# Seven block products for eight in the second down projection of a two-layer gated network (fp32, one NeuronCore)

## The chip, the cores and the metric

The kernel runs on one NeuronCore of a Trainium2 chip. The metric is the device time of one execution in microseconds; the time before is the median of three runs. The profile is one further execution, taken by the hardware profiler. Engines are named as in the profile: PE is TensorE, PEld its weight loads, DVE VectorE, ACT ScalarE, POOL GpSimd, SP the engine whose queue issues every DMA of this kernel.

## What is computed

An attention over 32 memory slots feeds a three-way maximum layer ("moe") and then a gated layer ("moe2"). The change lies in the gated layer alone, 4608 tokens, d_model 512, d_ff 1536:

```python
def _moe_ref(x, w1, w2, w3, w_out) -> np.ndarray:
    h = np.maximum(np.maximum(x @ w1, x @ w2), x @ w3)
    return (h @ w_out).astype(np.float32)
...
def _moe2_ref(x, w_gate, w_val, w_out) -> np.ndarray:
    gate = 1.0 / (1.0 + np.exp(-(x @ w_gate)))
    val = x @ w_val
    return (gate * val @ w_out).astype(np.float32)
```

All data are fp32.

## The kernel before

**Numbers.** Each fp32 operand of a large product is held as two fp32r tiles, a rounded part and what is left of it (`w_split`, L133: a ScalarE copy, then a subtraction on GpSimd or VectorE), and a product is three matmuls (`PASSES`, L333: low x high, high x low, high x high).

**First part (to about 568 us).** Attention, then the maximum layer, in four passes over pairs of batches. Its result x2 goes to DRAM (`x2_step`, L388). During the passes the weights of the gated layer are unpacked and kept in DRAM (`wbf`). In the last pass the first chunk's x and the first weights of the gated layer are prepared (L593 to L605).

**Second part: the gated layer.** Tokens go in five chunks (`SUPER`, L421), each of two halves of 512 tokens, in the last two chunks 384. For each chunk a loop over j (L776) takes the twelve column blocks of 128 of d_ff in six pairs, j and j + 6. The product of x (two halves of tokens, two halves of d_model) with the gate and value weights of such a pair is made in seven block products instead of eight (Strassen, in the form of Winograd): `x_sums` and `x_split` (L505, L515) make the seven left sides once per chunk, `t_make` (L460) makes the seven right sides from the weights in the first chunk and stores them in DRAM (`tbs`), `t_load` (L480) reads them in the later chunks. `up` (L724) makes one of the seven products for the gate (v = 0) or the value (v = 1) in PSUM, in the order 1, 6, 2, 7, 5, 4, 3, and the sums that belong to it. Each of the four blocks (c: half of the tokens, h: half of the pair) ends in `block_done` (L702): the sigmoid on ScalarE for the gate, gate x value on VectorE into `gf`, then a copy on ScalarE and a subtraction on GpSimd into the split tile `gg` (L720 to L722).

**The down projection.** `down` (L749) multiplies gg with w_out for 128 tokens at a time: two h, three passes, six matmuls with 128x128 weights (gg) and 512 columns (w_out) into one PSUM tile `po`. In the first j a ScalarE copy takes it to `acc`, in later j VectorE adds it to `acc`, and in the last j each 128x512 tile goes to `out`. So the sums over f are kept per 128 tokens, 8 or 6 tiles. w_out is split once per j in the first chunk (`wo_make`, L476), stored in `wos`, and loaded again later (`wo_load`, L484); it shares a ring of 11 buffers (`q4`, L419) with the seven right sides.

**Order.** The products of one j are run one j later, in between: after the third of the fourteen `up` calls each is followed by one `down` (L779 to L785). The preparation of the next weights stands behind each `up` pair, that of the next chunk's x in the last j of a chunk (L790 to L794). From this program order the framework's planner builds the order on each engine ahead of the run, by due times that it works out itself; it moves instructions past others where tiles and buffers allow. On the chip each engine then takes its own list in order, and SP its DMAs.

## Time and profile before

| | |
|---|---|
| median of 3 runs | 1390.36 us (1390.21 to 1392.23) |
| the profiled execution, as timed | 1393.86 us |
| its span, first to last instruction | 1392.1 us |
| mean granted TensorE clock | 0.984 |
| second part: first matmul to the end | 568.8 to 1392.1 us |
| gg @ w_out: matmuls, busy time of TensorE | 1296, 327.8 us |
| GpSimd on gg (120 operations) | 143.8 us |
| VectorE on acc (180 operations) | 124.3 us |

How to read the lines: a group is "line engine op, out<-in, shapes xcount | busy us, mean ns of one | idle time before them and what ended it". A line of the timeline begins with the start and the duration in us. A line of the waits has the total time, the number of waits and the longest. A line of the windows has, for each engine in the order PE, PEld, DVE, ACT, POOL, the busy time and the number of instructions in the window, then the granted clock, the share of the DMA engines and GB/s. Many operations are recorded at a helper's line: L73 is `sub`, L134 the copy in `w_split`; there the tiles tell what it is.

### The profile page before, as it was taken

Reading aid. Unit: us, or ns where it says so; the run is one execution under the profiler, and the core shown is the slowest. Engines: PE = TensorE matmul, PEld = TensorE weight load, DVE = VectorE, ACT = ScalarE, POOL = GpSimd, SP = SyncE. Lnnn points to the kernel's source line nnn. Section 1 sums busy time; section 2 is a strip of 40 time slices with the busy share of each in tenths; the row PEclk is TensorE's granted clock in tenths of the full one; section 3 lists DMA queues with packets and bytes.
Section 4 is the critical chain, followed back from the end, with each engine's and each line's share of the span. In section 5 each row is a group of like instructions: output and inputs, shape, how many; then the busy total and the mean of one; then the engine's idle time right before and its main releaser. Section 6 shows DMA issues by size and latency. Waiting matters only on the chain.

```text
span 1392.1 us, 22135 instructions
## 1 busy us (share of the span) xinstructions
PE 1338.2 (96%) x7864; PEld 1185.0 (85%) x7864; DVE 873.1 (63%) x1549; ACT 570.8 (41%) x1204; POOL 517.4 (37%) x454
## 2 busy tenths in 40 slices
PE   6588999999999999899999999999999999999998
PEld 3487899999999989688888888888888899999997
DVE  5999748976985897567765344454444544554454
ACT  5687546645654663353343321332222322133221
POOL 2776512331341228454486111371112711161111
PEclk8799999999999999999999999999999999999999
DMA  9588658767757745865556554465455666566661
GB/s 309 190 281 301 204 176 269 250 215 248 235 164 254 232 154 172 301 242 212 204 186 229 177 176 158 156 205 193 158 178 166 218 224 218 194 229 235 216 212 61
DMA packets 112271, 292.44 MB, mean 210 GB/s; under 512 B 12577, under 2 KB 28961, under 8 KB 112161
## 3 DMA queue, kind: packets, MB, share of 16 engines
q1 hardware_dynamic: 112160, 291.03, 62.1%
q8 instruction: 62, 1.02, 0.3%
q14 instruction: 49, 0.39, 0.1%
HBM read 224.92 MB, written 66.06 MB: 209 GB/s over the span
## 4 chain that ended last, share of the span: by engine, by line
PE 79%; DVE 10%; DMA 5%; issue 2%; ACT 2%; POOL 1%; SPq 0%; DVEq 0%; ACTq 0%; POOLq 0%
PE po L755 21%; PE px L688 16%; PE pz L688 11%; PE pv L688 10%; PE ps L393 8%; PE ps L370 8%; DVE g L73 2%; PE ps L343 2%; DVE ca L129 1%; DVE ca L128 1%; PE ps L209 1%; DVE hm L381 1%; DVE hm L382 1%; PE ps L246 1%; DVE ca L127 1%
## 5 line engine op out<-in xcount | busy, mean ns | idle before, releaser
L755 PE MATMUL po<-wo,gg 128*128 128x512 f32 x1296 | 327.8, 392 | 1.3 <-POOL gg L73 1.3
L73 POOL TENSOR_TENSOR gg<-gf,gg 128x512 fp32r<-128x512 f32 (+1 forms) x120 | 143.8, 1199 | 471.4 <-ACT gg L721 430.6
L755 PEld LDWEIGHTS po<-wo,gg 128*128 128x128 f32 x1296 | 242.4, 188 | 49.8 <-POOL gg L73 1.7
L370 PE MATMUL ps<-attn,g 128*128 128x288 f32 x1728 | 255.0, 301 | 19.4 <-DVE g L73 12.4
L370 PEld LDWEIGHTS ps<-attn,g 128*128 128x128 f32 x1728 | 243.3, 192 | 28.4 <-issue 11.4
L688 PE MATMUL px<-xa,tb 128*128 128x512 f32 (+1 forms) x1080 | 246.3, 370 | 6.2 <-DVE x L70 6.2
L767 DVE TENSOR_TENSOR acc<-po,acc 128x512 f32<-128x512 f32 x180 | 124.3, 690 | 176.5 <-PE po L755 176.3
L688 PEld LDWEIGHTS px<-xa,tb 128*128 128x128 f32 x1080 | 199.8, 189 | 34.9 <-issue 6.4
L688 PE MATMUL pv<-xa,tb 128*128 128x512 f32 (+1 forms) x720 | 169.2, 367 | 0.0
L688 PE MATMUL pz<-xa,tb 128*128 128x512 f32 (+1 forms) x720 | 169.2, 367 | 0.0
L73 POOL TENSOR_TENSOR h<-hm,h 128x288 fp32r<-128x288 f32 x96 | 83.6, 876 | 207.6 <-DVE h L70 105.6
L393 PE MATMUL ps<-h,wo 128*128 128x288 f32 x1152 | 159.1, 297 | 0.6 <-DVE hm L382 0.6
L393 PEld LDWEIGHTS ps<-h,wo 128*128 128x128 f32 x1152 | 155.3, 190 | 2.7 <-issue 1.9
L688 PEld LDWEIGHTS pz<-xa,tb 128*128 128x128 f32 x720 | 132.4, 188 | 18.8
L688 PEld LDWEIGHTS pv<-xa,tb 128*128 128x128 f32 x720 | 131.8, 188 | 17.7
L721 ACT CAST gg<-gf 128x512 fp32r<-128x512 f32 (+1 forms) x120 | 69.4, 578 | 177.8 <-DVE gf L717 132.4
L739 DVE TENSOR_TENSOR u<-pz,p 128x512 f32<-128x512 f32 (+1 forms) x120 | 76.3, 636 | 101.9 <-PE pz L688 97.8
L73 DVE TENSOR_TENSOR g<-ps,g 64x384 fp32r<-64x384 f32 x180 | 99.2, 552 | 33.2 <-ACT g L357 30.2
L711 ACT ACTIVATE sg<-sg 128x512 f32<-128x512 f32 (+1 forms) x90 | 53.1, 590 | 143.4 <-DVE sg L709 143.1
L357 ACT CAST g<-ps 64x384 fp32r<-64x384 f32 x192 | 90.6, 474 | 37.3 <-DVE g L73 22.9
L73 POOL TENSOR_TENSOR xa<-xf,xa 128x512 fp32r<-128x512 f32 (+1 forms) x64 | 79.3, 1261 | 21.4 <-ACT xa L134 18.7
L717 DVE TENSOR_TENSOR gf<-gf,sg 128x512 f32<-128x512 f32 (+1 forms) x90 | 72.3, 803 | 10.6 <-DVE gf L716 1.4
(92 smaller groups left out, 1402.4 us busy)
## 6 DMA issues: line engine op xcount, KB each, us to landing
tb<-tbs SPq DMA_DIRECT2D x168, 512.0 KB, 3.8
wx<-wxs SPq DMA_DIRECT2D x72, 384.0 KB, 4.0
wo<-wos SPq DMA_DIRECT2D x48, 512.0 KB, 5.0
tbs<-tb SPq DMA_DIRECT2D x42, 512.0 KB, 2.8
raw<-wb_dram SPq DMA_DIRECT2D x48, 384.0 KB, 3.6
kv<-kvm_dram SPq DMA_DIRECT2D x48, 256.0 KB, 4.8
raw<-wx_dram SPq DMA_DIRECT2D x24, 384.0 KB, 3.9
wxs<-wx SPq DMA_DIRECT2D x24, 384.0 KB, 4.3
```

The lines of the kernel that those rows point to most:

```text
L73: eng.tensor_tensor(out=o, in0=a, in1=b, op=ALU.subtract)
L343: pe.matmul(ps[:, :384], lhsT=vt[:, x, 2 * e:2 * e + 2].rearrange("p a m -> p (a m)"), rhs=w[:, y], start=(n == 0), stop=(n == 2),)
L357: act.copy(t[r, 0], ps[r, :384])
L370: pe.matmul(ps[w][:, :U], lhsT=G[b, j, g][:, x, 128 * w:128 * w + 128], rhs=at[:, y, hf * U:hf * U + U], start=(n == 0), stop=(n == 5),)
L393: pe.matmul(ps[:, :U], lhsT=wo1_t[:, x, (d * J + j) * 128:(d * J + j) * 128 + 128], rhs=H[u, j][:, y], start=(n == 0), stop=(n == 3 * J - 1),)
L688: pe.matmul(ps[:, :half], lhsT=w[:, a, o:o + 128], rhs=x[:, k, c, :half], start=(first and n == 0), stop=(n == 5), skip_group_check=not first,
L711: act.activation(out=sg, in_=src, func=AF.Sigmoid)
L717: vec.tensor_tensor(out=gf, in0=gf, in1=sg, op=ALU.mult)
L721: act.copy(t[:, 0, :half], gf)
L739: vec.tensor_tensor(out=u, in0=ps[:, :half], in1=E["p1", v], op=ALU.add)
L755: pe.matmul(ps, lhsT=GG[sc, j, c, h][:, x, 128 * m:128 * m + 128], rhs=WO[sc, j, h][:, y], start=(n == 0), stop=(n == 5),)
L767: vec.tensor_tensor(out=t, in0=ps, in1=t, op=ALU.add)
```

## The change

gg @ w_out is also done in seven block products: the pair of column blocks (h) is the inner dimension in two halves, tokens in the halves c, and d_model in two halves of 256 (`HD`). The left sides are made from the four `gf` blocks on GpSimd: block 1 is (0,0), block 4 is (1,1); when (1,0) is there, three sums make A22 + A21, A11 - A21 and the one for product 6, in place; when (0,1) is there, one more makes the one for product 3. Seven splits then make seven `gg` tiles (eight buffers, six before). The right sides are made in `wo_make` with four subtractions of 128x256 on VectorE and seven splits of 128x256 per j, kept in seven buffers of their own, stored in `wos` and reloaded one by one.

`down` makes one of the seven products for up to 256 tokens: per 128 tokens three matmuls with 256 columns, two such into one `po` bank. The seven sums over f are kept apart (`acc`, seven tiles of 128 x 4 x 256) through the six j of a chunk. Only in the last j are they joined, by seven additions on GpSimd (`BEFORE`), some ahead of the eviction that adds the last j's product; blocks 2, 3 and 4 are stored per eviction, block 5 after its last addition. There are fourteen `down` calls per j, one behind each `up`, in the order 1, 6, 7, 5, 4, 2, 3. The loading of w_out for the first chunk gets its own tile (`wv`), the ring of right sides shrinks from 11 to 8 buffers, and `u` of product 7 is written in place.

```diff
--- before.py
+++ after.py
@@ -76,7 +76,7 @@
     wxs = tc.dram_tile([J, 4, 128, 2, PC], F32, name="wxs")
     wbf = tc.dram_tile([NI, 128, 4 * PC], F32, name="wbf")
     tbs = tc.dram_tile([NI // 2, 7, 128, 2, DM], F32, name="tbs")
-    wos = tc.dram_tile([NI, 128, 2, DM], F32, name="wos")
+    wos = tc.dram_tile([NI // 2, 7, 128, 2, DM // 2], F32, name="wos")
 
     const = ctx.enter_context(tc.tile_pool(name="const", bufs=1))
     ident = const.tile([128, 128], F32, name="ident")
@@ -416,8 +416,13 @@
 
 
     NJ = NI // 2
-    NQ = 11
+    NQ = 8
     ORDER = (1, 6, 2, 7, 5, 4, 3)
+    DORDER = (1, 6, 7, 5, 4, 2, 3)
+    HD = DM // 2
     SUPER = []
     t0 = 0
     for half in (512, 512, 512, 384, 384):
@@ -430,15 +435,12 @@
 
     def tw_load(j):
 
-        def tile():
-            if j == 0:
-                return f32(q4_tile("tw"))
-            return b2.tile([128, 2, DM], F32, tag="tw", name="tw", bufs=3)
         for h, i in enumerate((j, j + NJ)):
-            t = TW[j, h] = tile()
+            t = TW[j, h] = b1.tile([128, 2, DM], F32, tag="tw", name="tw", bufs=2)
             dma(t.rearrange("p h c -> p (h c)"), wbf[i, :, 0:2 * DM])
-        t = TW[j, 2] = tile()
+    def wv_load(j):
+        t = TW[j, 2] = b1.tile([128, 2, DM], F32, tag="wv", name="wv", bufs=1)
         for h, i in enumerate((j, j + NJ)):
             dma(t[:, h], wbf[i, :, 2 * DM:3 * DM])
 
@@ -450,9 +452,8 @@
         sub(vec, t, a, b)
         return t
 
-    def kept(src, dst, name, eng):
-        t = q4_tile(name)
+    def kept(t, src, dst, eng):
         w_split(src, t[:, 0], t[:, 1], eng)
         dma(dst, f32(t))
         return t
@@ -471,20 +472,36 @@
         src = {1: B11, 2: B21, 3: B22, 6: TD.get(6)}.get(pr)
         if src is None:
             src = TD.pop(pr)
-        TB[0, j, pr] = kept(src, tbs[j, pr - 1], "tb", vec if pr in (2, 5) else pool)
-    def wo_make(j):
-        for h, i in enumerate((j, j + NJ)):
-            WO[0, j, h] = kept(TW[j, 2][:, h], wos[i], "wo2", vec if h else pool)
+        TB[0, j, pr] = kept(q4_tile("tb"), src, tbs[j, pr - 1], vec if pr in (2, 5) else pool)
+    def wo_tile():
+        return b1.tile([128, 2, HD], F32R, tag="wo2", name="wo2", bufs=7)
+    def wo_make(j, pr):
+        w = TW[j, 2]
+        B11, B12, B21, B22 = w[:, 0, :HD], w[:, 0, HD:], w[:, 1, :HD], w[:, 1, HD:]
+        if pr == 6:
+            sub(vec, B11, B12, B11)
+            TD["w"] = b1.tile([128, HD], F32, tag="wd", name="wd", bufs=1)
+            sub(vec, TD["w"], B22, B11)
+        elif pr == 7:
+            sub(vec, B12, B22, B12)
+        elif pr == 4:
+            sub(vec, TD["w"], B21, TD["w"])
+        src = {1: B11, 2: B21, 3: B22, 5: B11, 7: B12}.get(pr)
+        if src is None:
+            src = TD["w"]
+        WO[0, j, pr] = kept(wo_tile(), src, wos[j, pr - 1], vec if pr in (5, 2) else pool)
 
     def t_load(sc, j, pr):
         t = TB[sc, j, pr] = q4_tile("tb")
         dma(f32(t), tbs[j, pr - 1])
 
-    def wo_load(sc, j):
-        for h in range(2):
-            t = WO[sc, j, h] = q4_tile("wo2")
-            dma(f32(t), wos[j + h * NJ])
+    def wo_load(sc, j, pr):
+        t = WO[sc, j, pr] = wo_tile()
+        dma(f32(t), wos[j, pr - 1])
 
     XA = {}
     XR = {}
@@ -595,6 +612,7 @@
             br = tc.alloc_tile_pool(name="br", bufs=1, side="right", reuse_waits="tile")
             at(NS, x_load, 0)
             at(NS, tw_load, 0)
+            at(NS, wv_load, 0)
             at(NS + 1, x_sums, 0, 0)
             at(NS + 2, x_sums, 0, 1)
             at(NS + 2, t_make, 0, ORDER[0])
@@ -602,7 +620,8 @@
                 at(NS + 3 + n * 0.8, x_split, 0, pr, vec if n % 2 else None)
                 if n:
                     at(NS + 8 + n * 0.8, t_make, 0, pr)
-            at(NS + 14, wo_make, 0)
+            for n, pr in enumerate(DORDER):
+                at(NS + 13 + n // 3, wo_make, 0, pr)
         for j in range(2, J):
             for hp in range(4):
                 at(4 * (j - 2) + hp, w_step)
@@ -699,6 +718,13 @@
     def small(name, bufs):
         return b2.tile([128, 512], F32, tag=name, name=name, bufs=bufs)
 
+    F = {}
+    def gg_split(sc, j, pr, x):
+        half = SUPER[sc][1]
+        t = GG[sc, j, pr] = b2.tile([128, 2, 512], F32R, tag="gg", name="gg", bufs=8)
+        w_split(x, t[:, 0, :half], t[:, 1, :half])
     def block_done(sc, j, v, c, h, ps, other):
 
         half = SUPER[sc][1]
@@ -710,16 +736,28 @@
                 src = sg
             act.activation(out=sg, in_=src, func=AF.Sigmoid)
             return
-        gf = small("gf", 4)[:, :half]
+        gf = F[c, h] = small("gf", 4)[:, :half]
         sg = E.pop(("sg", c, h))
         if other is not None:
             vec.tensor_tensor(out=gf, in0=ps[:, :half], in1=other, op=ALU.add)
             vec.tensor_tensor(out=gf, in0=gf, in1=sg, op=ALU.mult)
         else:
             vec.tensor_tensor(out=gf, in0=ps[:, :half], in1=sg, op=ALU.mult)
-        t = GG[sc, j, c, h] = b2.tile([128, 2, 512], F32R, tag="gg", name="gg", bufs=6)
-        act.copy(t[:, 0, :half], gf)
-        sub(pool, t[:, 1, :half], gf, f32(t[:, 0, :half]))
+        if (c, h) == (0, 0):
+            gg_split(sc, j, 1, gf)
+        elif (c, h) == (1, 1):
+            gg_split(sc, j, 4, gf)
+        elif (c, h) == (1, 0):
+            A11, A22 = F[0, 0], F[1, 1]
+            pool.tensor_tensor(out=A22, in0=gf, in1=A22, op=ALU.add)
+            sub(pool, gf, A11, gf)
+            sub(pool, A11, A22, A11)
+            for pr, x in ((6, A11), (7, gf), (5, A22)):
+                gg_split(sc, j, pr, x)
+        else:
+            gg_split(sc, j, 2, gf)
+            sub(pool, gf, gf, F[0, 0])
+            gg_split(sc, j, 3, gf)
 
     def up(sc, j, pr, v):
         half = SUPER[sc][1]
@@ -735,8 +773,9 @@
             p1 = E["p1", v] = small("p1", 2)[:, :half]
             act.copy(p1, ps[:, :half])
         elif pr in (6, 7):
-            u = E["u", pr, v] = small(f"u{pr}", 2)[:, :half]
-            vec.tensor_tensor(out=u, in0=ps[:, :half], in1=E["p1", v], op=ALU.add)
+            p1 = E["p1", v]
+            u = E["u", pr, v] = p1 if pr == 7 else small("u6", 2)[:, :half]
+            vec.tensor_tensor(out=u, in0=ps[:, :half], in1=p1, op=ALU.add)
         elif pr == 2:
             block_done(sc, j, v, 0, 0, ps, None)
         elif pr == 5:
@@ -746,42 +785,70 @@
         else:
             block_done(sc, j, v, 0, 1, ps, E["u", 6, v])
 
-    def down(sc, j, c, m):
+    def add(sc, x, y):
+        n = SUPER[sc][1] // 128
+        a, b = ACC[sc, x][:, :n], ACC[sc, y][:, :n]
+        pool.tensor_tensor(out=a, in0=a, in1=b, op=ALU.add)
+    BLOCK = {2: (0, 0), 3: (0, 1), 4: (1, 0), 5: (1, 1)}
+    def store(sc, pr, m0, m1):
         t0, half = SUPER[sc]
-        ps = psB.tile([128, DM], F32, tag="po", name="po", bufs=2)
-        n = 0
-        for h in range(2):
-            for x, y in PASSES:
+        c, d = BLOCK[pr]
+        r0 = t0 + c * half
+        dma(out[r0 + 128 * m0:r0 + 128 * m1, d * HD:d * HD + HD].rearrange("(m p) d -> p m d", p=128),
+            ACC[sc, pr][:, m0:m1])
+    BEFORE = {1: ((2, 1),), 7: ((7, 6), (4, 7)), 6: ((6, 1),), 5: ((3, 5), (3, 6), (5, 7))}
+    def down(sc, j, pr, q):
+        n = SUPER[sc][1] // 128
+        m0, m1 = 2 * q, min(2 * q + 2, n)
+        ps = psB.tile([128, 2, HD], F32, tag="po", name="po", bufs=2)
+        for m in range(m0, m1):
+            for n, (x, y) in enumerate(PASSES):
                 pe.matmul(
-                    ps,
-                    lhsT=GG[sc, j, c, h][:, x, 128 * m:128 * m + 128],
-                    rhs=WO[sc, j, h][:, y],
-                    start=(n == 0), stop=(n == 5),
+                    ps[:, m - m0],
+                    lhsT=GG[sc, j, pr][:, x, 128 * m:128 * m + 128],
+                    rhs=WO[sc, j, pr][:, y],
+                    start=(n == 0), stop=(n == 2),
                 )
-                n += 1
         if j == 0:
-            t = ACC[sc, c, m] = b2.tile([128, DM], F32, tag="acc", name="acc", bufs=8)
-            act.copy(t, ps)
+            if q == 0:
+                ACC[sc, pr] = b2.tile([128, 4, HD], F32, tag="acc", name="acc", bufs=7)
+            act.copy(ACC[sc, pr][:, m0:m1], ps[:, :m1 - m0])
         else:
-            t = ACC[sc, c, m]
-            vec.tensor_tensor(out=t, in0=ps, in1=t, op=ALU.add)
+            t = ACC[sc, pr][:, m0:m1]
+            vec.tensor_tensor(out=t, in0=ps[:, :m1 - m0], in1=t, op=ALU.add)
+        if j == NJ - 1 and pr in (2, 3, 4):
+            store(sc, pr, m0, m1)
+        if q == 0:
+            return
         if j == NJ - 1:
-            r0 = t0 + c * half + m * 128
-            dma(out[r0:r0 + 128, :], t)
+            for x, y in BEFORE.get(pr, ()):
+                add(sc, x, y)
+            if pr == 5:
+                store(sc, 5, 0, SUPER[sc][1] // 128)
+        if (sc, j) != LAST:
+            nxt = after(sc, j)
+            if nxt[0] == 0:
+                wo_make(nxt[1], pr)
+            else:
+                wo_load(*nxt, pr)
 
     tw_load(1)
+    wv_load(1)
     downs = []
     for sc in range(len(SUPER)):
         nxt = sc + 1 < len(SUPER)
         for j in range(NJ):
             if nxt and j == NJ - 2:
                 x_load(sc + 1)
-            slot = 0
             for pr in ORDER:
                 for v in range(2):
                     up(sc, j, pr, v)
-                    slot += 1
-                    if slot >= 3 and downs:
+                    if downs:
                         down(*downs.pop(0))
                 if sc == 0 and j + 1 < NJ:
                     t_make(j + 1, pr)
@@ -792,14 +859,12 @@
                         x_sums(sc + 1, 0)
                         x_sums(sc + 1, 1)
                     x_split(sc + 1, pr)
-            if sc == 0 and j + 1 < NJ:
-                wo_make(j + 1)
-                if j + 2 < NJ:
-                    tw_load(j + 2)
-            elif (sc, j) != LAST:
-                wo_load(*after(sc, j))
+            if sc == 0 and j + 2 < NJ:
+                tw_load(j + 2)
+            if sc == 0 and 0 < j < NJ - 1:
+                wv_load(j + 1)
             assert not downs
-            downs = [(sc, j, c, m) for c in (1, 0) for m in range(SUPER[sc][1] // 128)]
+            downs = [(sc, j, pr, q) for pr in DORDER for q in range(2)]
     for x in downs:
         down(*x)
```

## The prediction

> **What bounds the kernel now.** I read the page's totals first, then the table of windows over the second layer (from 568.8 us to the end), then TensorE's waits, then single groups and stretches of the timeline.
>
> ```profile
> span 1392.1 us, 22135 instructions
> PE 1338.2 (96%) x7864; PEld 1185.0 (85%) x7864; DVE 873.1 (63%) x1549; ACT 570.8 (41%) x1204; POOL 517.4 (37%) x454
> ```
>
> ```profile
> core 0: us, PE busy (x) PEld busy (x) DVE busy (x) ACT busy (x) POOL busy (x), PEclk, DMA share, GB/s
> 600.00:714.00 114.00, 114.00 (x503) 94.09 (x502) 78.17 (x103) 45.97 (x78) 58.08 (x44) 1.00 0.53 194
> 719.00:749.00 30.00, 30.00 (x134) 24.79 (x133) 15.84 (x21) 12.00 (x21) 27.68 (x22) 1.00 0.76 262
> 800.00:900.00 100.00, 100.00 (x441) 82.58 (x440) 48.57 (x73) 22.74 (x38) 21.57 (x18) 1.00 0.51 168
> 1378.00:1392.00 14.00, 9.02 (x39) 6.86 (x38) 6.21 (x10) 1.49 (x3) 2.02 (x2) 1.00 0.30 113
> ```
>
> ```profile
> PE px L688 <- DVE x L70: 6.2, 1, 6.2
> PE po L755 <- POOL gg L73: 1.3, 1, 1.3
> ```
>
> TensorE is busy without a gap in the windows from 600 to 900, at the full granted clock, and in the whole second layer it waits twice: 6.2 us where it begins, 1.3 us in the last products. So every matmul saved counts there, as long as the other engines can still follow. They are far from full between the chunk ends (window 800 to 900: VectorE 49%, GpSimd 22%), but the window from 719 to 749, the last j of the first chunk, has GpSimd at 27.68 of 30 us already, and from 600 to 714, where weights are made, VectorE stands at 78.17 of 114.
>
> **The saving on TensorE.** The products gg @ w_out are now 48 matmuls of 512 columns per j in a chunk of half 512 (36 at half 384): 18 x 48 + 12 x 36 = 1296, the count of the row below. Seven block products take 7 x 4 x 3 = 84 (63) matmuls of 256 columns: 18 x 84 + 12 x 63 = 2268. Columns fall to 7/8, instructions rise by three quarters, so the fixed part of a matmul decides.
>
> ```profile
> L755 PE MATMUL po<-wo,gg 128*128 128x512 f32 x1296 | 327.8, 392 | 1.3 <-POOL gg L73 1.3
> ...
> L73 POOL TENSOR_TENSOR gg<-gf,gg 128x512 fp32r<-128x512 f32 (+1 forms) x120 | 143.8, 1199 | 471.4 <-ACT gg L721 430.6
> ```
>
> ```profile
> 524.32 38.24 PE L393 MATMUL ps<-h,wo 128*128 128x288 f32 x288
> ```
>
> ```profile
> 1376.26 2.25 PE L688 MATMUL pv<-xa,tb 128*128 128x384 f32 x12
> ```
>
> The mean of 392 ns overlaps with its neighbours; the spacing is what costs. At 512 columns the window 800 to 900 gives 100 / 441 = 0.2268 us. At 288 columns a run of 288 matmuls lasts 38.24 us, 0.1328 each. At 384, twelve last 2.25 us; less the last one's own 0.334 (mean of its group), that is 1.916 / 11 = 0.1742.
>
> ```profile
> L688 PE MATMUL px<-xa,tb 128*128 128x384 f32 x432 | 83.9, 336 | 0.0
> L688 PE MATMUL pz<-xa,tb 128*128 128x384 f32 x288 | 59.7, 334 | 0.0
> ...
> L73 POOL TENSOR_TENSOR gg<-gf,gg 128x384 fp32r<-128x384 f32 x48 | 48.8, 1016 | 201.7 <-ACT gg L721 201.7
> ```
>
> No matmul of this kind with 256 columns is in the trace. From 384 to 288 a column costs 0.0414 / 96 = 0.00043 us, so 32 columns less than 288 give 0.1328 - 0.0138 = 0.119. Its bounds are 0.1328 (nothing gained below 288: the weight load of 128 columns could be the floor) and 0.1328 x 256 / 288 = 0.118. I take 0.119, since the three points lie nearly on a line. Before: 1296 x 0.2268 = 293.9 us; after: 2268 x 0.119 = 269.9. **-24**, between -26 and +7.
>
> The Trainium skill, "TensorE: Matmul & The Clock Gate", section "Back-to-back issue gap", gives N / 2.4 + 2.5 ns for a warm isolated matmul, 109 ns at 256 columns; the products would then take 248 us, a saving of 46. At 288 and 512 columns the rule gives 122.5 and 215.8 against 132.8 and 226.8 here, so this trace has some 10 ns more per matmul.
>
> **The last products.** Now the last x @ W matmul ends at 1376.26 + 2.25 = 1378.5, 36 products follow, and 1392.1 is the end: 13.6 us.
>
> ```profile
> 1377.54 0.56 DVE L717 TENSOR_TENSOR gf<-gf,sg 128x384 f32<-128x384 f32 x1
> ...
> 1380.89 1.02 POOL L73 TENSOR_TENSOR gg<-gf,gg 128x384 fp32r<-128x384 f32 x1 [1.09 <-ACT gg L721]
> ...
> 1388.40 0.69 DVE L767 TENSOR_TENSOR acc<-po,acc 128x512 f32<-128x512 f32 x1 [0.68 <-PE po L755]
> ```
>
> After the change GpSimd has, from the moment block (1,0) is there (1378.1): three sums of blocks, five of the seven splits' subtractions (those of block 1 and 4 come earlier) and one sum for block 3, 9 operations of 1.016 us, 9.1 us; and then the seven adds that join the sums over f, 128x768 each. By the two gg rows an operation costs 1.296 us at 512 (a row for that alone stands below), 1.016 at 384, so 0.28 per 128 columns: 1.86 at 768, 13.0 for seven. GpSimd is free again at 1378.1 + 22.1 = 1400.2. What ends now after the last VectorE add (1389.1 to 1392.1, 3.0 us of store) must still follow: 1403.2, 24.7 us after the last x @ W where it was 13.6. Of the saving of 24, 36 x 0.2268 - 63 x 0.119 = 0.7 lay in this stretch where TensorE no longer decides. **+12**; bounds +8, if adds slip into gaps or a smaller last step ends it, and +16, if GpSimd waits for ScalarE's copies between its steps.
>
> **Iterations that make weights (first chunk).** Per j at half 512, x @ W takes 84 x 0.2268 = 19.05 us, the products 10.9 before and 84 x 0.119 = 10.0 after: 29.9 and 29.05.
>
> ```profile
> L767 DVE TENSOR_TENSOR acc<-po,acc 128x512 f32<-128x512 f32 x24 | 16.5, 687 | 13.8 <-PE po L755 13.8
> L717 DVE TENSOR_TENSOR gf<-gf,sg 128x512 f32<-128x512 f32 x12 | 13.6, 1129 | 1.3 <-ACT sg L711 0.9
> ...
> L73 DVE TENSOR_TENSOR td<-tw,td 128x512 f32<-128x512 f32 x7 | 9.2, 1321 | 0.1
> ...
> L73 DVE TENSOR_TENSOR td<-tw 128x512 f32<-128x512 f32 x6 | 5.2, 868 | 4.0 <-DMA tw<-wbf 4.0
> L73 DVE TENSOR_TENSOR wo<-tw,wo 128x512 fp32r<-128x512 f32 x4 | 4.7, 1169 | 1.3 <-ACT wo L134 1.3
> ```
>
> ```profile
> L73 POOL TENSOR_TENSOR tb<-td,tb 128x512 fp32r<-128x512 f32 x12 | 16.5, 1373 | 18.8 <-ACT tb L134 18.8
> ...
> L73 POOL TENSOR_TENSOR wo<-tw,wo 128x512 fp32r<-128x512 f32 x4 | 6.1, 1514 | 0.0
> ```
>
> ```profile
> L717 DVE TENSOR_TENSOR gf<-gf,sg 128x512 f32<-128x512 f32 x15 | 10.4, 693 | 1.9 <-DVE gf L716 0.5
> ```
>
> ```profile
> L717 DVE TENSOR_TENSOR gf<-gf,sg 128x512 f32<-128x512 f32 x3 | 3.9, 1302 | 0.4 <-ACT sg L711 0.2
> ```
>
> ```profile
> L73 POOL TENSOR_TENSOR gg<-gf,gg 128x512 fp32r<-128x512 f32 x20 | 25.9, 1296 | 117.0 <-ACT gg L721 96.5 <-PE po L755 20.5
> ```
>
> The three L717 rows are one operation, both inputs in SBUF, in three windows: 693 ns where GpSimd is mostly idle (930 to 1080), 1129 at 58 of 114 us (600 to 714 of the windows), 1302 at 27.7 of 30 (719 to 749). The two engines slow each other on such operations; L767, which reads PSUM, stays at 687. So VectorE per j: 78.17 / 114 x 29.9 = 20.5 us now; six more evictions (14 for 8) 4.1; one split of w_out less, -1.2; four differences and two splits of 256 columns, 0.43 to 0.66 each by half the td rows, 3.3; nine operations slowed by a further 0.2, 1.8. That is 28.5 of 29.05. GpSimd: five tb splits 6.9, eleven operations on gf and gg at 1.296 (four now) 14.3, five w_out splits at 1.296 - 0.56 = 0.74, 3.7: 24.9, and some 2 more for the mutual slowing. Both engines are within 2 us of TensorE's own time, each waiting for the other at several places. I charge 1.5 us for each of the four j that have it: **+6**, bounds 0 and 20 (the port rival below).
>
> **Chunk ends.** In the last j of a chunk GpSimd also prepares the next x, and in the next j it makes the seven adds, of 1024 columns now: 1.296 + 4 x 0.28 = 2.42 us, 16.9 together. VectorE's evictions of products 4, 2 and 3 wait for adds, and behind a waiting eviction stand the evictions that free TensorE's PSUM banks. First end: 27.7 (row 719 to 749) + 7 x 1.296 + 3.7 = 40.5, then 16.9 + 14.3 = 31.2: 71.7 for 58.1 us of TensorE, 13.6 too much. Second, without w_out: 10. Third and fourth (x of 384 columns, 18 operations left in that window's 22 at 1.016, then iterations of 84 x 0.1742 + 63 x 0.119 = 22.1 us): 32.6 + 28.1 for 51.2 and 29.5 + 24.2 for 44.2, about 9.5 each. Sum 43 too much. How much reaches TensorE?
>
> ```profile
> 803.37 1.75 PE L688 MATMUL pz<-xa,tb 128*128 128x512 f32 x7
> 804.96 1.54 PE L755 MATMUL po<-wo,gg 128*128 128x512 f32 x6
> 806.33 1.29 PE L688 MATMUL pz<-xa,tb 128*128 128x512 f32 x5
> ```
>
> The code asks for 6 and 6 around the products; the built order has 7 and 5. So x @ W is moved ahead of products that aren't ready, and each j has 19 us of it; the four gf buffers and two PSUM buffers of po stop that run after about 10 us. With that cover I charge a quarter, **+11**: 5 at the first end, 2 at each other. Bounds 0 and 43.
>
> **The rest.** At the start seven w_out pieces pass through ACT, GpSimd and the store queue where two did, beside the last x2 stores:
>
> ```profile
> 568.16 0.46 DVE L70 COPY x<-ps 128x288 f32<-128x288 f32 x1 [3.86 <-DMA x2s<-x]
> ```
>
> That copy, late because of a store, is what TensorE waits 6.2 us for; a queue with five more stores ahead of it can make it later: +1, bounds 0 and 5. Weight loads: 7 x 256 KB per j for 2 x 512 KB, 18 MB more in all, at a DMA share of 0.51 to 0.76; each has a whole j (22 us or more) to land against the 5.0 us of the row below, so nothing; without that cover they would cost their landing. ScalarE's three more copies per j stay under half of its time.
>
> ```profile
> wo<-wos SPq DMA_DIRECT2D x48, 512.0 KB, 5.0
> ```
>
> **Sum:** -24 + 12 + 6 + 11 + 1 = +6 on the profiled execution: span 1392.1, and 1393.9 as it was timed; that run lies 3.5 above the median of the runs shown, 1390.4, to which I add the same difference: **1396.4**.
>
> **The rivals.**
> - *Hidden (faster).* The order built ahead moves enough x @ W in front, and only the tail and the start remain: -24 + 12 + 1 + 1 for stray waits = -10: 1380.4. For it: not one wait in 800 us now, though GpSimd stood at 92% at a chunk end. Against: afterwards it stands above 100% over two j together.
> - *Port-bound first chunk (slower).* If GpSimd is nearly always at work, each of VectorE's operations with both inputs in SBUF waits half a GpSimd operation, 0.65: nine at 1.34 (12.1), six of 256 columns at about 1.1 (6.5), and 25 that read PSUM at 0.687 (17.2): 35.8 per j, 6.8 over TensorE, in three j (20). -24 + 12 + 20 + 11 + 1 = +20: 1410.4. It decides once GpSimd passes 90% there; I have 24.9 + 2 of 29.05. The skill's "SBUF — State Buffer", section "SBUF: two separate sides", has this as a lock in which the loser blocks for the whole instruction; 693 against 1302 ns agrees with waiting of that size.
> - *Chunk ends paid in full.* -24 + 12 + 6 + 43 + 1 = +38: 1428. It needs TensorE to stand still whenever GpSimd is behind, against the 19 us of other matmuls.
> - *No gain below 288 columns.* 2268 x 0.1328 = 301.2, +7; an iteration of half 512 is then 1.2 us longer, so the overloads shrink to about 2 and 8: 7 + 12 + 2 + 8 + 1 = +30: 1420.
> - *Ten ns less per matmul*, 0.109: 247.2, -47; iterations shorter by 0.8 raise the overloads to 9 and 14: -47 + 12 + 9 + 14 + 1 = -11: 1379.4. The gap rule above says this; against it stand the spacings at three widths.
>
> That the products don't shrink at all can't be: the counts follow from the code.
>
> **How the numbers follow.** Forecast 0.40, hidden 0.34, port 0.12, chunk ends in full 0.05, no gain below 288 0.05, ten ns less 0.04. Around the forecast's +6 the charges move it by some 6 either way: of its 0.40, 0.03 falls faster, 0.09 within 0.2% (2.8 us, about what can be told from no change), 0.28 slower. Hidden gives 0.32 faster and 0.02 the same. Faster 0.03 + 0.32 + 0.04 = 0.39, same 0.11, slower 0.50. The range goes from 1377 to 1411, leaving out the two dear rivals and the outer half of the two fast ones; the forecast's own range is 1388 to 1406.
>
> **What would show it.** Right: po matmuls spaced 0.117 to 0.121; TensorE's waits in the first chunk and after each chunk end on POOL (gg) or on evictions of VectorE, some 17 us in all; an end 23 to 26 us after the last x @ W, with GpSimd's adds on the chain. Wrong: a spacing near 0.133; GpSimd over 90% with no idle TensorE; a tail under 20 us; DMA as releaser of TensorE.

## The result and the profile after

The changed kernel takes 1437.14 us (median of 4 runs, 1434.6 to 1437.85) against 1391.3 before: ratio 1.033, interval 1.0315 to 1.0344. It is 46 us slower. The forecast had the sign, with +6; its range ended at 1411.

The page of the changed kernel, then its windows. The first row lies in the first chunk. The second is the first j of the next chunk, in which the first chunk's last products run. The third lies between two chunk ends, and the fourth is the end of the run.

```profile
span 1435.2 us, 25150 instructions
...
PE 1335.6 (93%) x8836; PEld 1217.5 (85%) x8836; DVE 992.6 (69%) x1749; ACT 632.8 (44%) x1358; POOL 867.5 (60%) x723
```

```profile
600.00:714.00 114.00, 103.90 (x552) 88.32 (x551) 91.36 (x114) 51.70 (x102) 95.69 (x73) 0.99 0.60 211
744.00:780.00 36.00, 33.49 (x193) 28.90 (x191) 30.32 (x39) 10.30 (x21) 36.00 (x30) 1.00 0.55 178
...
800.00:900.00 100.00, 99.67 (x561) 86.89 (x560) 51.58 (x75) 34.51 (x60) 60.62 (x44) 1.00 0.66 215
...
1399.00:1435.00 36.00, 22.25 (x136) 19.06 (x134) 18.39 (x35) 4.00 (x8) 24.56 (x19) 0.90 0.35 110
```

GpSimd is at work all of the 36 us from 744 to 780, as forecast for a chunk end, and for 95.69 of 114 us in the first chunk. But the last row is the dear one: 36 us in which TensorE still has 136 matmuls to start, where the kernel before had 14 us and 39. The waits of TensorE (total, number, longest):

```profile
PE po L811 <- DVE acc L823: 16.6, 23, 4.5
...
PE px L707 <- DVE x L70: 8.4, 1, 8.4
PE po L811 <- issue: 8.2, 15, 1.3
PE po L811 <- POOL gg L73: 8.0, 4, 5.4
PE pz L707 <- DVE u L778: 4.4, 3, 2.0
```

The products (po) wait most for evictions (acc), and half as long for GpSimd; for 8.2 us of their waits the profile names no releaser ("issue"). What such a wait looks like, in the timeline of TensorE near the end, two calls (nine matmuls) in a row:

```profile
1413.68 1.30 PE L811 MATMUL po<-wo,gg 128*128 128x256 f32 x9 [0.48 <-issue]
1415.46 1.29 PE L811 MATMUL po<-wo,gg 128*128 128x256 f32 x9 [0.48 <-issue]
1417.24 1.30 PE L811 MATMUL po<-wo,gg 128*128 128x256 f32 x9 [0.48 <-issue]
1419.01 1.30 PE L811 MATMUL po<-wo,gg 128*128 128x256 f32 x9 [0.48 <-issue]
```

A pair of calls every 1.77 us, though its matmuls are worth 9 x 0.1175 = 1.06. VectorE's rows in the same stretch show why: it starts when the first tile's six matmuls are done, needs 1.02 us for both evictions, and then waits itself for 0.75. The eviction of a full tile takes 0.69 of the 1.02, so the one that starts at 1414.67 ends at 1415.36, and TensorE's next call starts at 1415.46. From these times I read the "issue" waits as waits for that eviction.

```profile
1414.67 1.02 DVE L823 TENSOR_TENSOR acc<-po,acc 128x512 f32<-128x512 f32 x2 [0.75 <-PE po L811]
1416.44 1.02 DVE L823 TENSOR_TENSOR acc<-po,acc 128x512 f32<-128x512 f32 x2 [0.75 <-PE po L811]
1418.22 1.02 DVE L823 TENSOR_TENSOR acc<-po,acc 128x512 f32<-128x512 f32 x2 [0.75 <-PE po L811]
```

Neither engine is full; with two buffers they take turns. Then GpSimd's seven adds come in one row:

```profile
1417.55 12.62 POOL L791 TENSOR_TENSOR acc<-acc 128x768 f32<-128x768 f32 x7 [1.78 <-DVE acc L823]
```

To see where time is lost I add up, over all successive matmuls of the gated layer, the distance from start to start less 0.2268, 0.1735 or 0.1175 us for 512, 384 or 256 columns (what runs without a wait show), by stretch. A distance counts to the stretch of the matmul from which it starts, so the wait of 1.3 us before, right behind the last x @ W, stands in chunk 5.

| us lost by TensorE | before | after |
|---|---|---|
| start of the gated layer | 6.4 | 8.6 |
| first chunk | 3.1 | 21.9 |
| chunks 2, 3, 4, 5 | 0.5, 0.5, 1.0, 2.4 | 13.0, 4.5, 7.0, 15.0 |
| after the last x @ W | 0.2 | 16.6 |
| sum | 14 | 87 |

So 73 us more are lost and 2268 x 0.1175 - 1296 x 0.2268 = -27 us of matmuls saved: +46 by this count, where the two spans differ by 43. The 2.2 us at the start are most of that difference: the first matmul of the gated layer starts at 568.8 us before and at 568.9 after, so they aren't in the spans. After the last x @ W 138 matmuls of products are left; the code's order would leave 66, and before it was 36 of 36.

### The profile page after: what moved, and what is told of

The parts are those of the page before. It is cut to its first block, busy times and chain, and to the rows that moved or that the text cites. A ratio compares the mean times of both kernels' runs of the same rounds, so it can differ in the third digit from the quotient of the medians.

```text
span 1435.2 us, 25150 instructions
## 1 busy us (share of the span) xinstructions
PE 1335.6 (93%) x8836; PEld 1217.5 (85%) x8836; DVE 992.6 (69%) x1749; ACT 632.8 (44%) x1358; POOL 867.5 (60%) x723
## 4 chain that ended last, share of the span: by engine, by line
PE 64%; DVE 11%; POOL 9%; DMA 7%; issue 6%; ACT 3%; SPq 0%; DVEq 0%; POOLq 0%; ACTq 0%
PE po L811 14%; PE px L707 13%; PE pz L707 8%; PE pv L707 8%; PE ps L370 8%; PE ps L393 8%; POOL gg L73 2%; PE ps L343 2%; DVE acc L823 2%; DVE g L73 2%; POOL gf L73 1%; POOL xa L73 1%; PE ps L209 1%; PE ps L246 1%; DMA tb<-tbs 1%
## 5 line engine op out<-in xcount | busy, mean ns | idle before, releaser
L73 POOL TENSOR_TENSOR gg<-gf,gg 128x512 fp32r<-128x512 f32 (+1 forms) x210 | 257.2, 1238 | 191.0 <-ACT gg L134 141.8
L811 PE MATMUL po<-wo,gg 128*128 128x256 f32 x2268 | 324.3, 285 | 35.9 <-DVE acc L823 16.6
L811 PEld LDWEIGHTS po<-wo,gg 128*128 128x128 f32 x2268 | 305.2, 191 | 60.0 <-DVE acc L823 25.1
L823 DVE TENSOR_TENSOR acc<-po,acc 128x512 f32<-128x512 f32 x350 | 216.0, 633 | 171.2 <-PE po L811 160.8
L707 PE MATMUL px<-xa,tb 128*128 128x512 f32 (+1 forms) x1080 | 259.6, 373 | 11.7 <-DVE x L70 8.4
L370 PEld LDWEIGHTS ps<-attn,g 128*128 128x128 f32 x1728 | 243.4, 192 | 29.7 <-issue 11.1
L707 PEld LDWEIGHTS px<-xa,tb 128*128 128x128 f32 x1080 | 193.9, 190 | 35.6 <-issue 8.7
L134 ACT CAST gg<-gf 128x512 fp32r<-128x512 f32 (+1 forms) x210 | 115.9, 578 | 226.8 <-PE po L811 115.9
L707 PE MATMUL pz<-xa,tb 128*128 128x512 f32 (+1 forms) x720 | 173.0, 369 | 7.1 <-DVE u L778 4.4
L73 POOL TENSOR_TENSOR gf<-gf 128x512 f32<-128x512 f32 (+1 forms) x90 | 108.8, 1209 | 4.5
L743 DVE TENSOR_TENSOR gf<-gf,sg 128x512 f32<-128x512 f32 (+1 forms) x90 | 89.4, 993 | 3.5 <-ACT sg L737 1.7
```

The costliest lines, as they stand in the source:

```text
L73: eng.tensor_tensor(out=o, in0=a, in1=b, op=ALU.subtract)
L134: act.copy(hi, w)
L370: pe.matmul(ps[w][:, :U], lhsT=G[b, j, g][:, x, 128 * w:128 * w + 128], rhs=at[:, y, hf * U:hf * U + U], start=(n == 0), stop=(n == 5),)
L707: pe.matmul(ps[:, :half], lhsT=w[:, a, o:o + 128], rhs=x[:, k, c, :half], start=(first and n == 0), stop=(n == 5), skip_group_check=not first,
L743: vec.tensor_tensor(out=gf, in0=gf, in1=sg, op=ALU.mult)
L811: pe.matmul(ps[:, m - m0], lhsT=GG[sc, j, pr][:, x, 128 * m:128 * m + 128], rhs=WO[sc, j, pr][:, y], start=(n == 0), stop=(n == 2),)
```

## The experiments

Theories: **A**, the built order lets the products lag behind x @ W; **B**, GpSimd is overloaded and TensorE waits for it; **C**, two PSUM buffers of po against an eviction per 0.7 us of matmuls; **D**, what C leaves is GpSimd's queue at the chunk ends; **E**, the first chunk stalls on making w_out. Every time is a median against the kernel before on the same chip (1390.6 to 1390.9).

**The order held.** Every matmul of the gated layer goes through the framework's call that keeps program order.

```diff
-                pe.matmul(
+                tc.keep_in_program_order(pe.matmul(
```

> The changed kernel with every matmul of the gated layer held in program order (one product call behind each x @ W call); nothing else is different. Theory A (the built order lets the products lag: 138 of them, not 63, are left after the last x @ W, and when they run in a row each pair of calls takes 1.735 us for 1.06 us of matmuls): 66 are left, so the end shrinks by about 72 x 0.193 = 14 us and the stalls in the chunks get fewer: 1405 to 1423 us. Theory B (GpSimd is overloaded, TensorE waits for it in the end): the order only moves the waits, TensorE stops for gg after each chunk end: 1437 us or more. Theory C (two PSUM buffers of po against an eviction per 0.7 us of matmuls is the cost): with a product call behind each x @ W call the evictions are hidden: 1415 to 1425, and no wait of a product for an eviction outside the end.

Measured: 1473.75 us, ratio 1.060 (1.058 to 1.062). 66 matmuls are left at the end, but

```profile
PE po L811 <- POOL gg L73: 56.7, 15, 16.3
```

Theory A alone falls, and theory C's figure for this run is missed by 50 us. The stretch after the last x @ W is 26.1 us instead of 36.5, so the lag costs; but the run ahead of x @ W that goes with it hides GpSimd's lateness, which shows here as 57 us of waits. For B this is only half a yes, since the next run has as many operations on gf and gg on GpSimd.

**GpSimd's load alone**, in the kernel before:

```diff
         sub(pool, t[:, 1, :half], gf, f32(t[:, 0, :half]))
+        for _ in range({(0, 0): 0, (1, 1): 0, (1, 0): 5, (0, 1): 2}[c, h]):
+            d = small("dm", 1)[:, :half]
+            sub(pool, d, gf, f32(t[:, 0, :half]))
```

> The kernel before with seven further GpSimd subtractions per j (into a scratch tile, reading gf and gg): GpSimd has 11 operations on gf and gg per j as in the changed kernel, TensorE the old products and the old order. Theory B (GpSimd's load by itself): 15 to 40 us slower than before, 1406 to 1431. Theory A: the old order has no lag, GpSimd stays behind without anyone waiting: 1391 to 1396.

Measured: 1394.97 us, ratio 1.0038 (1.0023 to 1.0052): 4 us for seven more operations per j. Load by itself isn't it; it must stand in the way of something.

**Without sums and adds.**

```diff
-            pool.tensor_tensor(out=A22, in0=gf, in1=A22, op=ALU.add)
-            sub(pool, gf, A11, gf)
-            sub(pool, A11, A22, A11)
...
-            sub(pool, gf, gf, F[0, 0])
...
-            for x, y in BEFORE.get(pr, ()):
-                add(sc, x, y)
```

> The changed kernel without the four sums of gf blocks per j and without the seven adds of acc at each chunk end (the products are of unsummed blocks and the output is not joined). GpSimd loses 4 of 11 operations per j and 77 us of adds. Theory B: most of the loss goes: 1437 - 13 at the end - 30 in the chunks, 1385 to 1400 us. Theory A: the built order still leaves 147 products after the last x @ W; only the adds on the end's chain go (12.6 us of GpSimd there, partly beside products): 1418 to 1430.

Measured: 1407.02 us, ratio 1.012 (1.011 to 1.014). This lies between the ranges of A and B. 30 us go, but it is 16 us slower than before although TensorE has 27 us less to do, and 147 matmuls are left at the end. Something is lost that has nothing to do with GpSimd's sums.

**More buffers in the end only.**

```diff
+        tag = "po"
+        if (sc, j) == LAST:
+            late["n"] += 1
+            tag = ("po", "px", "pz", "pv")[late["n"] % 4]
-        ps = psB.tile([128, 2, HD], F32, tag="po", name="po", bufs=2)
+        ps = psB.tile([128, 2, HD], F32, tag=tag, name="po", bufs=2)
```

> The changed kernel, but the last j's 14 product calls take their PSUM tiles in turn from the eight banks of po, px, pz and pv instead of two. Theory C: these 7 pairs run at VectorE's 1.1 us instead of 1.735: 7 x 0.65 = 4 to 5 us less, 1432 to 1433. Theory B: the adds on GpSimd end the run all the same, 12.6 us in a row after the last sums: 1437 within 1.5.

Measured: 1436.87 us, ratio 1.0335 (1.030 to 1.037): no change that these runs can tell (the four lie between 1432 and 1441). In the trace TensorE loses 5.5 us after the last x @ W instead of 16.6, but that stretch still lasts 35.4 us, not 36.5: with the products quicker, the adds end it.

**Eight products in the same short calls.** The kernel before, without Strassen, with one PSUM tile per h:

```diff
-        ps = psB.tile([128, DM], F32, tag="po", name="po", bufs=2)
         for h in range(2):
+            ps = psB.tile([128, DM], F32, tag="po", name="po", bufs=2)
+            for d in range(2):
...
+                        ps[:, 256 * d:256 * d + 256],
```

> The kernel before, its eight block products kept, but made in calls of 256 columns: one PSUM tile and one eviction for each block of 128 tokens and each h (6 matmuls of 256 columns, 0.7 us) instead of one for both h (6 of 512, 1.37 us). No sums, no seven w_out pieces, no further GpSimd work. The matmuls alone cost 2592 x 0.1175 - 1296 x 0.2268 = +11 us. Theory C (an eviction of VectorE per 0.7 us of matmuls over two po buffers makes the products lag and stall): 198 products are left after the last x @ W and run at 0.19 each; 1420 to 1440 us. Theory B (what costs is the work on GpSimd): +11 only, 1400 to 1406.

Measured: 1451.18 us, ratio 1.043 (1.041 to 1.044), 198 matmuls left at the end: more than either range. Of the 60 us, 11 are the matmuls. The rest shows that short calls over two buffers are a loss with no sum, no w_out piece and no add of Strassen's. But it isn't lost at the end as theory C had it: 6.5 us are lost after the last x @ W and some 43 in chunks 2 to 5, and there the waits name mostly the loads of the x @ W weights:

```profile
PE pz L688 <- DMA tb<-tbs: 20.3, 20, 2.6
PE po L755 <- DVE acc L766: 2.6, 12, 0.6
```

In this kernel w_out shares a ring of 11 buffers with these weights, so products that lag would hold buffers that the loads need. That is argued from the code; in the changed kernel, where w_out has its own buffers, such waits are 2.7 us.

**Three buffers for po**; pz and pv, of which one is begun when the other ends, share three.

```diff
-            E["z", v] = psB.tile([128, 512], F32, tag="pz", name="pz", bufs=2)
+            E["z", v] = psB.tile([128, 512], F32, tag="pzv", name="pz", bufs=3)
...
-            E["v", v] = psB.tile([128, 512], F32, tag="pv", name="pv", bufs=2)
+            E["v", v] = psB.tile([128, 512], F32, tag="pzv", name="pv", bufs=3)
...
-        ps = psB.tile([128, 2, HD], F32, tag="po", name="po", bufs=2)
+        ps = psB.tile([128, 2, HD], F32, tag="po", name="po", bufs=3)
```

> The changed kernel with three PSUM buffers for po instead of two; pz and pv share three in place of two each. Theory C: in the built order 72 products are left after the last x @ W instead of 138, and the lag falls between the chunk ends; the end loses 66 x 0.19 = 13 us, the chunks 10 to 25: 1395 to 1415. Theory B: GpSimd has the same work and TensorE waits for gg instead: 1430 to 1440.

Measured: 1411.41 us, ratio 1.014 (1.013 to 1.016): 26 us less than the changed kernel, with 72 matmuls left at the end. Theory C holds for these 26. By the count of lost time, 15.0 of them are in chunk 5, 5.4 after the last x @ W, 6 in chunks 2 to 4 and none in the first chunk. Four buffers for po, and one ring of four (tag `pu`) for all of px, pz and pv:

> The changed kernel with four po buffers; px, pz and pv share four. Theory C: like three po buffers or some us better, 1390 to 1412, if x @ W with four buffers instead of six does not begin to wait for its own evictions; then 1410 to 1430. Theory B: 1430 to 1440.

Measured: 1415.12 us, ratio 1.017 (1.015 to 1.019): the third buffer is what counts, a fourth, paid for by x @ W, isn't worth it. And the control, the same exchange in the kernel before:

> The kernel before with the same exchange of PSUM buffers (three po, three shared by pz and pv). Its built order had no lag: no change beyond 2 us, 1389 to 1393. If the shared ring by itself is good or bad for x @ W, that shows here.

Measured: 1391.42 us, ratio 1.0003 (0.9994 to 1.0013). The eight products of 256 columns with the same exchange:

> The eight block products in calls of 256 columns, now with three po buffers: in the built order 72 are left at the end instead of 198. If two buffers against the short calls were the whole loss of that kernel beyond its matmuls, what is left is +11 us of matmuls and 2 to 6 at the start and the end: 1401 to 1409. If evictions on VectorE as such cost, 1415 or more.

Measured: 1401.34 us, ratio 1.008 (1.006 to 1.010): the 11 us of its matmuls and nothing else. The list of what TensorE waits for from its first x @ W on is down to one line:

```profile
PE po L755 <- POOL gg L73: 1.8, 1, 1.8
```

**Three buffers, and neither sums nor adds** (both diffs above).

> Both together: three po buffers, and without the four sums per j and the seven adds at each chunk end (the products are of unsummed blocks, the output is not joined). If buffers and GpSimd's sums are all that costs, what is left is the saving of 27 us on TensorE less some 10 for the start, the first chunk and the end: 1370 to 1385. Above 1400 there is a third cause.

Measured: 1374.64 us, ratio 0.988 (0.986 to 0.990). So C and the sums and adds together hold 62 of the 46 + 27 = 73 us. Which of the two holds the 37? The sums' four lines alone, then the adds' two:

> The changed kernel with three po buffers, without the four sums of gf blocks per j (the products are of unsummed blocks). The two together (sums and adds) were worth 1411 - 1375 = 37 us. If the sums hold most (they stand on the way from the last blocks of a j to five of its seven products, in every j): 1380 to 1390. If the adds hold most: 1400 to 1408.

> The changed kernel with three po buffers, without the seven adds at each chunk end (the output is not joined). If the adds hold most of the 37 us (the end alone 12, the other chunk ends 3 to 5 each): 1385 to 1395. If the sums do: 1400 to 1408. Both short of the sum of 37 means that each alone still overfills GpSimd.

Measured: 1390.48 us without the sums (ratio 0.9996, 0.998 to 1.001), 21 less than with them; 1398.8 without the adds (1.006, 1.004 to 1.007), 13 less. 21 + 13 = 34 of 37: nearly independent. The sums hold the larger part, though 1398.8 lies in neither of the two ranges.

**Work moved from GpSimd to VectorE**, with three buffers: first the adds, then also the splits of gg 2 and 4 after the first chunk.

```diff
-        pool.tensor_tensor(out=a, in0=a, in1=b, op=ALU.add)
+        vec.tensor_tensor(out=a, in0=a, in1=b, op=ALU.add)
...
-        w_split(x, t[:, 0, :half], t[:, 1, :half])
+        w_split(x, t[:, 0, :half], t[:, 1, :half], vec if sc and pr in (2, 4) else pool)
```

> The changed kernel with three po buffers, and the seven adds at a chunk end on VectorE instead of GpSimd. Theory D (with three buffers, what is left of the loss is GpSimd's queue at the chunk ends and in the end): at 384 columns VectorE needs 0.56 for GpSimd's 1.02, so an add of 768 about 1.0 for 1.86; the end loses 6 us, the chunk ends some 5: 1398 to 1404. If the dependence of the products on the sums, not GpSimd's queue, holds the end: 1408 to 1412.

> As the run with adds on VectorE, and the splits of gg 2 and 4 after the first chunk subtract on VectorE too, so GpSimd has 9 operations per j instead of 11. Theory D: another 2 to 6 us at the chunk ends: 1394 to 1402. If VectorE (70% busy, slowed on operations with both inputs in SBUF) becomes the late one: 1402 to 1412.

Measured: 1412.45 (ratio 1.016, 1.014 to 1.017) and 1408.75 us (1.013, 1.0115 to 1.0145) against 1411.41. Theory D falls, as far as it was put as a matter of GpSimd's queue: an add takes 1.49 us on VectorE in the median where it took 2.39 on GpSimd, and the stretch after the last x @ W is 22.6 us instead of 25.2, but the chunks before lose that again (the second 13.2 us instead of 11.1, the fifth 3.0 instead of 0, against 3.1 instead of 6.3 in the fourth). The second time lies in the range put down for a late VectorE. Leaving the adds out gains 13, moving them nothing: they stand between evictions that wait for them, whichever engine does them. That this order of adds and evictions is the reason was only argued.

**w_out in the first chunk**, with three buffers: seven pieces by two copies on ScalarE each.

```diff
-        WO[0, j, pr] = kept(wo_tile(), src, wos[j, pr - 1], vec if pr in (5, 2) else pool)
+        t = WO[0, j, pr] = wo_tile()
+        act.copy(t[:, 0], src)
+        act.copy(t[:, 1], src)
+        dma(wos[j, pr - 1], f32(t))
```

> The changed kernel with three po buffers, in which the first chunk makes the seven w_out pieces without differences and by two copies on ScalarE each (the pieces are not the right ones; four subtractions on VectorE and seven on GpSimd and VectorE per j are left out). Theory E (the first chunk stalls because making w_out adds work to VectorE and GpSimd): its 22 us of lost time fall to 10 or less: 1396 to 1403. If the first chunk stalls by the sums and splits of gg alone: 1409 to 1413.

Measured: 1391.24 us, ratio 1.0006 (0.9996 to 1.0016): 20 less. The first chunk loses 7.8 us instead of 21.9; the next chunk, into which its lateness runs over, 4.1 instead of 11.1. In the windows of two j of the first chunk with three buffers and the whole w_out, VectorE is at 91% and 94%:

```profile
650.00:688.00 38.00, 32.03 (x179) 26.16 (x178) 34.41 (x45) 14.15 (x29) 28.69 (x23) 1.00 0.52 189
688.00:722.00 34.00, 31.47 (x182) 27.06 (x182) 32.02 (x44) 13.59 (x28) 33.12 (x26) 1.00 0.57 204
```

The share alone doesn't tell: without w_out's work VectorE is busy for 37.07 of 38 us in the first of these windows, and TensorE for 37.88. Theory E holds by the time and the lost time. The run also leaves out the two splits of w_out per j that the kernel before has. This 20 isn't to be added to the 37: without sums the first chunk also finds GpSimd free, and loses 11.3 us in that run.

No version here with the whole of the computation and seven products beats the kernel before; the best is 1408.75.

## Why the prediction was wrong in its size

- **The saving, right.** 256-column matmuls follow each other at 0.118 us (forecast 0.119), -27 us instead of -24; here nine take 1.06 us from start to the next start:

```profile
1268.48 1.22 PE L811 MATMUL po<-wo,gg 128*128 128x256 f32 x9
1269.54 0.34 PE L707 MATMUL pv<-xa,tb 128*128 128x384 f32 x1
```

  The Trainium skill's rule in "TensorE: Matmul & The Clock Gate", section "Back-to-back issue gap", gives 0.109 at 256 columns. The trace has 9 ns more, about as at 288 and 512 columns.
- **The step that failed is one that the prediction didn't take: "six more evictions (14 for 8) 4.1".** It counted evictions as time on VectorE, and put at nothing that each of them also frees a PSUM buffer; the two buffers of po it named only as what stops the run ahead of x @ W. A product call fell from 1.37 to 0.71 us of matmuls, its eviction stayed at 0.69, the buffers stayed two. In the built order the products then lag behind the code's order by up to 156 matmuls (30 before), and by 162 even without GpSimd's sums and adds; with three buffers it is 72. Where no x @ W is there to run beside them, a pair of calls takes 1.77 us for 1.06. Of the 40 us between +6 and +46, the third buffer gives back 26. That two buffers are too few for these short calls is shown twice, on the changed kernel and on eight products of 256 columns (50 us), though there much of it came by way of weight loads. That the planner defers a call whose buffer isn't free and never catches up in a TensorE-bound stretch fits the counts; how it weighs them was not looked into.
- **The cover, half wrong.** The prediction charged a quarter of GpSimd's excess because x @ W is moved ahead. It is, and without that 57 us of waits for gg show. But work that was run ahead isn't there at the end: 138 matmuls and 36.5 us after the last x @ W, where 66 and 26.1 us are left when the order is held.
- **The last products, right once the buffers are set right.** Forecast 24.7 us from the last x @ W to the end (+12); 36.5 in the changed kernel, 25.2 with three buffers, 12.8 without sums and adds too. With three buffers GpSimd's last 16 operations, nine on gf and gg and seven adds, go from 1384.7 to 1406.4, 21.7 us where the prediction had 22.1. Its mechanism isn't the whole of it: the seven adds on a faster engine shorten the stretch by 2.6 us only, where 6 were expected.
- **The first chunk, mis-sized.** +6 was charged, with its upper bound of 20 in the port rival; 19 us more are lost there (21.9 less 3.1), 13 more than charged, and leaving out w_out's work gives 20. The six operations of 256 columns were taken at 0.55 us each, by halving full-width rows. They measured 0.78 to 1.22:

```profile
L73 DVE TENSOR_TENSOR wv<-wv 128x256 f32<-128x256 f32 x6 | 6.7, 1114 | 3.8 <-POOL wo L73 3.8
...
L73 DVE TENSOR_TENSOR wo<-wv,wo 128x256 fp32r<-128x256 f32 x5 | 3.9, 777 | 2.2 <-ACT wo L134 2.2
L73 DVE TENSOR_TENSOR wd<-wv 128x256 f32<-128x256 f32 x3 | 3.7, 1224 | 0.1
```

  In the same window (600 to 714 of the changed kernel) VectorE's subtractions of 512 columns took 0.86 to 1.35 us, so half the width saved little, though it takes an eviction from PSUM from 0.68 to 0.41. The Trainium skill's "SBUF — State Buffer", section "SBUF: two separate sides", states a lock: of an operation of VectorE with two SBUF inputs and one of GpSimd that reads SBUF, the first to start keeps the shared ports for its whole instruction, and the other waits. That a short operation then waits as long as a wide one is my reading; the rows agree with it. The prediction named the lock in a rival and then scaled the rows by width in the sum. Its sign for that rival, GpSimd over 90%, did not come: GpSimd was busy for 84% of that window, and about the rival's 20 us were lost all the same. Making w_out is shown to be what the first chunk stalls on; that these widths are the reason is argued.
- **Chunk ends, about right.** With three buffers chunks 2 to 5 lose 18.5 us where 4.4 were lost before, +14 against +11. With two buffers they lose 39.5, +35: it is in this term most of all that the missing step shows.
- **The start, right in kind:** 8.6 us lost, 6.4 before, on the same copy (L70), but the 2.2 us between them aren't in the difference of the spans.

## What to carry to other kernels

When a change makes a matmul group shorter, compare the group's time with the time until its PSUM buffer is free again, not only the evicting engine's share of the span: in the last 36 us here TensorE was 62% and VectorE 51% busy, and they took turns. Work that TensorE runs ahead to hide a late producer is a loan, and the stretch after the last such work shows it. Price an operation of VectorE that runs beside a busy GpSimd by a row of its own width taken there, and not by half of a wider row: the 256-column ones took 0.78 to 1.22 us here, where half had given 0.55.

## What the runs showed of the hardware that I had not expected

- Halving an eviction saves 0.27 of 0.68 us (timeline of VectorE in the changed kernel, shortly before the last x @ W):

```profile
1395.91 0.68 DVE L823 TENSOR_TENSOR acc<-po,acc 128x512 f32<-128x512 f32 x1
...
1396.97 0.41 DVE L823 TENSOR_TENSOR acc<-po,acc 128x256 f32<-128x256 f32 x1
```

- TensorE's granted clock fell behind waits, and not in the short runs of products. In the changed kernel it is 1.00 where pairs of calls take turns with evictions (1411 to 1424), and 0.66 where products go on after waits of 1.30 and 0.73 us (1403 to 1408) and after one of 3.58 us (1427 to 1432):

```profile
1403.00:1408.00 5.00, 4.07 (x19) 3.55 (x18) 2.50 (x6) 0.51 (x1) 4.02 (x4) 0.66 0.40 103
1411.00:1424.00 13.00, 9.49 (x67) 8.05 (x65) 7.16 (x14) 1.03 (x2) 10.00 (x8) 1.00 0.26 80
1427.00:1432.00 5.00, 4.01 (x18) 3.46 (x18) 2.68 (x6) 0.00 (x0) 3.16 (x2) 0.66 0.57 190
```

  Nine matmuls take 1.29 us before the longer wait, and 1.76 and 2.26 behind it:

```profile
1422.52 1.29 PE L811 MATMUL po<-wo,gg 128*128 128x256 f32 x9 [0.43 <-DVE acc L823]
1427.39 1.76 PE L811 MATMUL po<-wo,gg 128*128 128x256 f32 x9 [3.58 <-DVE acc L823]
1429.33 2.26 PE L811 MATMUL po<-wo,gg 128*128 128x256 f32 x9 [0.19 <-issue]
```

  With three buffers the last 25 us, which also hold waits of 3.5 and 1.9 us, have a mean of 0.77:

```profile
1385.00:1410.00 25.00, 11.63 (x72) 10.33 (x70) 9.31 (x19) 2.26 (x5) 21.26 (x16) 0.77 0.26 85
```

  So an end that waits for adds also slows what is left of its matmuls. How long a wait must be for this stays open: behind one of 1.25 us, at 1302.9 in the changed kernel, the clock stayed at 1.00.
